# Half-length power tables, a last tile in two column halves, and the turning of six chunks of k moved from TensorE to the DMA queue

**Chip, cores, metric.** One core of one Trainium2 chip. The metric is device time of one execution in microseconds (us), given as the median of the runs of one kernel. Everything here is one core; over 1.5% above the fastest of the same kernel counts as slow. Runs of one batch ran on the same chip, beside runs of the kernel before.

## The reference, cut to what matters

```python
def _attn_ref(r, k, v, w, u):            # r, k, v: (4, 8, 768, 48) float32; w, u: (8, 48)
    for t in range(S):
        cur = einsum('bhd,bhe->bhde', u[None] * kt, vt)
        y[:, :, t] = einsum('bhd,bhde->bhe', rt, state + cur)
        state = w[None, :, :, None] * state + einsum('bhd,bhe->bhde', kt, vt)
# then, on x = y as (4, 768, 384):  x + relu(layernorm(x) * g @ w1) @ w2      (w1: 384 x 1536)
```

The recurrence is done in 24 chunks of 128 tokens. Within a chunk, r is scaled by rising powers of w and k by falling ones, so that one masked score product per chunk takes the place of the recurrence. For this the kernel makes tables of powers of w at its start. An MLP over each chunk ("tile") follows and gives TensorE most of its work.

## The kernel before: the parts that matter

The tables are made by scans (a running product), turned on TensorE, and copied to `Fr` (two tables for r) and `Fk` (for k):

```python
T = const.tile([P, CK, 2 * L], FP32, name="T")          # CK = 3, L = 128
T2 = const.tile([P, CK, L], FP32, name="T2")
ones = const.tile([P, L], FP32, name="ones")
w_r = const.tile([P, CK], FP32, name="w_r")
...
for kc in range(CK):
    powers(T[:, kc, L + 1 : 2 * L], w_c, kc)             # scan of 127
    nc.scalar.copy(out=T[:, kc, 0:L], in_=T[:, kc, L : 2 * L])
nc.vector.reciprocal(out=w_r[:], in_=w_c[:])
for kc in range(CK):
    powers(T2[:, kc], w_r, kc)                           # scan of 128
```

`const` is the first of several pools of tiles. The pools lie one behind the other on each partition, every tile rounded up to 32 bytes. The tiles that loads write come behind `const`:

```python
dst = (k_t if what == "k" else vf_t)[i] = ld.tile([P, H, D], FP32, name=what)
...
eng.dma_start(out=dst[:], in_=src[b, :, s0 : s0 + L, :].rearrange("h t d -> t h d"))   # 192-byte pieces
```

k is scaled, turned by four TensorE transposes, and copied out of PSUM; a routine that does the same by a DMA is there but not used (`KP = 24`). The order of all work is made at build time by a small list scheduler that gets a duration for each task; each engine then works in that fixed order. SyncE (SP) issues nearly all DMAs in its own fixed order: loads, stores, and the turns of the normalized tile `xn`.

```python
if i < KP:   # TK: 4 transposes on TensorE, then kT: a copy on ScalarE (or VectorE)
else:
    add(f"kT{i}", "SP", 1.25, lambda i=i: transpose_k_by_dma(i), [f"sck{i}"], ..., lands=3.0)
```

Of the kernel before, what the change touches and what calls it, by code (L numbers as in the profile page):

```python
# [9 lines left out]
FP32 = mybir.dt.float32  # L10
# [116 lines left out]
def kernel(  # L127
# [12 lines left out]
    nc = tc.nc  # L140
# [130 lines left out]
    T = const.tile([P, CK, 2 * L], FP32, name="T")  # L271
    T2 = const.tile([P, CK, L], FP32, name="T2")
    nc.vector.memset(T[:, :, L : L + 1], 1.0)
    ones = const.tile([P, L], FP32, name="ones")
    nc.vector.memset(ones[:], 1.0)
    w_r = const.tile([P, CK], FP32, name="w_r")

    def powers(out, base, kc):
        nc.vector.tensor_tensor_scan(
            out=out,  # L280
            data0=base[:, kc : kc + 1].to_broadcast([P, out.shape[1]]),
            data1=ones[:, : out.shape[1]],
            initial=1.0,
            op0=ALU.mult,
            op1=ALU.mult,
        )
# [5 lines left out]
    nc.vector.tensor_copy(out=w_c[:], in_=wps[:, :CK])  # L292
    for kc in range(CK):
        powers(T[:, kc, L + 1 : 2 * L], w_c, kc)
        nc.scalar.copy(out=T[:, kc, 0:L], in_=T[:, kc, L : 2 * L])
    nc.vector.reciprocal(out=w_r[:], in_=w_c[:])
    for kc in range(CK):
        powers(T2[:, kc], w_r, kc)
# [4 lines left out]
    LH = L // 2  # L303
    for j in range(3):
        fps = ps_h.tile([P, 512], FP32, name="hp") if j < 2 else ps.tile([P, 512], FP32, name="y")
        for kc in range(CK):
            src = T2[:, kc] if j == 2 else T[:, kc, j : 2 * L : 2]
            nc.tensor.transpose(out=fps[:, kc * P : (kc + 1) * P], in_=src, identity=ident_f[:])
        src = fps[:, :C].rearrange("p (h d) -> p h d", h=H)
        nc.scalar.copy(out=Fr[:, j] if j < 2 else Fk[:], in_=src)  # L310
# [89 lines left out]

    def evacuate_r(i, eng):
        e, c = divmod(i, 2)
        rT_t[i] = trp.tile([P, HP, P], BF16, name="rT", bufs=NRT)
        (eng.copy if eng is nc.scalar else eng.tensor_copy)(  # L404
            out=rT_t[i][:].rearrange("p q (t j) -> p q j t", j=2),
            in_=tp_t[e][:, :, c * LH : (c + 1) * LH].rearrange("p (j q) t -> p q j t", j=2),
        )
# [43 lines left out]
    def bonus_copy(i):  # L451
        cc_t[i] = sb2.tile([P, H], FP32, name="cc")
        nc.scalar.copy(out=cc_t[i][:], in_=s_t[i][:, C : C + H])  # L453
# [138 lines left out]
    KP = 24  # L592
# [19 lines left out]
    def ln_evacuate(i):  # L612
        g, j = tile_group[i]
        nc.scalar.copy(out=xT_t[g][:, :, j * P : (j + 1) * P], in_=tp_t[i][:, :CK, :])
# [62 lines left out]

    plan = Planner(
# [5 lines left out]
    add("scan", "DVE", 5.65, None, pri=99)  # L684
    add("Fr", "ACT", 5.9, None, pri=99)
    add("Fk", "ACT", 0.65, None, needs=["Fr"], pri=99)
# [36 lines left out]
    for i in range(NT):  # L723
# [8 lines left out]
        if not half:  # L732
            add(f"scrb{e}", "", 0.0, None, [], [("scr", e, 1)], pri=p0)
            for t in range(2):
                add(f"scr{e}{t}", "POOL", 1.1, lambda g, e=e, t=t: scale_r(e, t, g), [f"r{e}", "Fr", f"scrb{e}"], [],
                    [("r", e)], pri=p0, alt=[("DVE", 0.7)])
            add(f"TR{e}", "PE", 0.46, lambda e=e: transposes_r(e), [f"scr{e}0", f"scr{e}1"], [("tr", ("r", e), 2)],
# [7 lines left out]
        else:  # L745
            add(f"kT{i}", "SP", 1.25, lambda i=i: transpose_k_by_dma(i), [f"sck{i}"], [("kT", i, 2)], [("sck", i)], pri=80,
                load=0.67, lands=3.0)
# [11 lines left out]
        add(f"cp{i}", "ACT", 0.2, lambda i=i: bonus_copy(i), [f"cc{i}"], [("cc", i, 1)], [("s", i)], pri=p0 + 1)  # L759
# [32 lines left out]
        if i < LNP:  # L792
            add(f"ln{i}", "PE", 0.18, lambda i=i: ln_transposes(i), [f"xn{i}", f"xT{g}"], [("tr", ("l", i), 1)],
                [("xn", i)], pri=p0 + 2)
            add(f"lc{i}", "ACT", 0.5, lambda i=i: ln_evacuate(i), [f"ln{i}"], [], [("tr", ("l", i))], pri=p0 + 2)
        else:
            add(f"lc{i}", "SP", 1.2, lambda i=i: ln_by_dma(i), [f"xn{i}", f"xT{g}"], [], [("xn", i)], pri=90, load=0.5, lands=3.0)
        for m in range(NM):
# [55 lines left out]
```

## Time and profile before

| | before |
|---|---|
| median of 3 runs | 159.12 us (158.75 to 160.19) |
| span of the profiled run, granted clock | 155.6 us, 1.00 |
| TensorE busy from 7 to 91 us, while loads run | 80.0 of 84 us |
| TensorE busy from 91 to 124 us | 32.91 of 33 us |
| DMA share from 7 to 91 us / from 91 on | about 1.0 / 0.3 and less |

The page has two regimes. As long as loads run, the DMA engines are full and TensorE has holes, partly filled with dummy products (`keep_warm` in the code, 8.3 us of busy time between 7 and 33; what they do to the clock is not shown). Once the loads are done, TensorE is the bound and every microsecond of it counts. The lines for this are in the prediction.

### The profile page before, as it was taken

The page shows a single profiled execution, that of the slowest core. Times are in us where ns is not written, and L with a number is a line of the kernel's source. Part 1 is how long each engine was busy: PE and PEld are TensorE (multiplying, and loading weights), DVE is VectorE, ACT ScalarE, POOL GpSimd, SP SyncE. Part 2 cuts the span into 40 slices and gives each one's busy share as a digit, 9 for nine tenths or more (in the row PEclk, how much of TensorE's full clock was granted, in tenths as well). Part 3 has the DMA queues.
Part 4 walks back from the last instruction along what each step waited for, and adds up shares of the span by engine and source line. Part 5 has one row for each costly group of instructions (what it writes and reads, how often), then busy time and mean ns, then how long its engine had stood idle before and what let it go on. Part 6 is the DMA issues. An engine that isn't in the chain of part 4 may idle for free.

```text
span 155.6 us, 4634 instructions
## 1 busy us (share of the span) xinstructions
PE 146.1 (94%) x1851; PEld 114.7 (74%) x1851; DVE 116.7 (75%) x232; ACT 97.4 (63%) x217; POOL 86.1 (55%) x116
## 2 busy tenths in 40 slices
PE   5999999989999999989899969999999999999990
PEld 5789898858886787757668757787887777777650
DVE  5879999978898999888989779898989731101231
ACT  3577888967869576737977458676575554463100
POOL 7379697687829976795794849953542120000000
PEclk9999999999999999999999999999999999999999
DMA  4999999998999999999999969212121220111122
GB/s 101 239 235 326 355 183 274 377 242 188 250 218 244 218 215 184 233 219 185 196 220 191 208 112 228 78 30 76 44 62 51 80 71 5 51 55 51 51 101 101
DMA packets 75418, 25.46 MB, mean 164 GB/s; under 512 B 69632, under 2 KB 74246, under 8 KB 75398
## 3 DMA queue, kind: packets, MB, share of 16 engines
q1 hardware_dynamic: 72070, 23.21, 64.9%
q10 hardware_dynamic: 3232, 1.97, 4.1%
q8 instruction: 14, 0.23, 0.7%
q14 instruction: 6, 0.05, 0.1%
q0 software_dynamic: 96, 0.01, 0.1%
HBM read 18.88 MB, written 4.72 MB: 152 GB/s over the span
## 4 chain that ended last, share of the span: by engine, by line
PE 60%; DVE 12%; DMA 11%; issue 5%; POOL 5%; ACT 4%; SPq 1%; POOLq 0%; DVEq 0%; ACTq 0%
PE o L654 22%; PE hp L627 20%; DMA wst<-in_moe_w_ch_dram 6%; DMA v<-in_v_dram 5%; PE at L422 3%; PE o L268 3%; PE hp L654 3%; DVE A L432 2%; PE tr L399 2%; DVE x L538 2%; PE tr L384 2%; PE y L525 2%; POOL Vb L457 1%; POOL sc L369 1%; DVE w_sb L350 1%
## 5 line engine op out<-in xcount | busy, mean ns | idle before, releaser
L627 PE MATMUL hp<-xT,w_sb 128*128 128x256 bf16 (+1 forms) x540 | 57.6, 251 | 0.7 <-DMA xT<-xn 0.6
L654 PE MATMUL o<-w_sb,hT 128*128 128x384 bf16 x264 | 52.1, 326 | 0.0
L627 PEld LDWEIGHTS <-w_sb 128*128 128x128 bf16 x540 | 43.5, 98 | 8.2 <-DMA xT<-xn 0.8
L641 ACT ACTIVATE hT<-hp 128x512 bf16<-128x512 f32 x60 | 35.5, 598 | 18.0 <-PE hp L627 17.5
L654 PEld LDWEIGHTS <-hT 128*128 128x128 bf16 x288 | 26.2, 98 | 13.0
L664 DVE SCALAR_TENSOR_TENSOR ot<-o,rs,x 128x384 f32<-128x384 f32 x22 | 13.5, 612 | 22.2 <-PE o L654 22.2
L432 DVE TENSOR_TENSOR A<-at,mask 128x1024 bf16<-128x1024 f32 x24 | 29.2, 1215 | 0.5 <-PE at L422 0.5
L457 POOL TENSOR_TENSOR Vb<-v,cc 128x384 f32<-128x384 f32 x24 | 20.8, 867 | 8.3 <-ACT cc L453 8.3
L369 POOL TENSOR_TENSOR sc<-r,Fr 128x384 bf16<-128x384 f32 x18 | 20.1, 1125 | 7.1 <-ACT Fr L310 2.7
L366 POOL TENSOR_TENSOR sc<-k,Fk 128x384 bf16<-128x384 f32 x19 | 19.8, 1041 | 0.1
L388 ACT COPY kT<-tr 128x512 bf16<-128x512 bf16 x22 | 12.9, 586 | 4.7 <-PE tr L384 3.3
L565 ACT ACTIVATE sq<-x,sum 128x384 bf16<-128x384 f32 x24 | 14.6, 609 | 1.7 <-DVE x L538 1.6
L538 DVE SCALAR_TENSOR_TENSOR x<-y,Vb 128x384 f32<-128x384 f32 x24 | 13.2, 548 | 1.9 <-POOL Vb L457 1.6
L404 ACT COPY rT<-tr 128x512 bf16<-128x512 bf16 x17 | 11.8, 738 | 4.1 <-PE tr L399 2.5
L268 PE MATMUL o<-ident 128*128 128x128 bf16 x152 | 12.1, 233 | 1.6 <-DVE ident L243 1.6
L268 PEld LDWEIGHTS <-ident 128*128 128x128 bf16 x152 | 9.9, 104 | 1.9 <-DVE ident L243 1.6
L422 PE MATMUL at<-rT,kT 48*128 48x128 bf16 x192 | 9.5, 219 | 1.7 <-ACT kT L388 1.5
L643 DVE TENSOR_SCALAR hT<-hp 128x512 bf16<-128x512 f32 x12 | 8.2, 687 | 1.8 <-PE hp L627 1.7
L384 PE MATMUL tr<-ident,sc 128*128 128x128 bf16 x92 | 8.9, 219 | 0.5 <-DVE rT L404 0.5
L422 PEld LDWEIGHTS <-kT 48*128 48x128 bf16 x192 | 5.4, 94 | 5.4 <-ACT kT L388 3.2
L525 PE MATMUL y<-vv,A 128*128 128x48 bf16 x192 | 8.7, 183 | 0.4 <-DVE A L432 0.4
L556 ACT ACTIVATE xn<-x,sum 128x384 bf16<-128x384 f32 x13 | 8.0, 618 | 1.6 <-DVE x L538 1.4
(87 smaller groups left out, 193.3 us busy)
## 6 DMA issues: line engine op xcount, KB each, us to landing
r<-in_r_dram SPq DMA_DIRECT2D x12, 384.0 KB, 4.6
k<-in_k_dram SPq DMA_DIRECT2D x24, 192.0 KB, 4.4
wst<-in_moe_w_ch_dram SPq DMA_DIRECT2D x6, 768.0 KB, 7.2
v<-in_v_dram SPq DMA_DIRECT2D x22, 192.0 KB, 3.9
out_dram<-ot SPq DMA_DIRECT2D x16, 192.0 KB, 2.7
out_dram<-ot ACTq DMA_DIRECT2D x8, 192.0 KB, 1.9
v<-in_v_dram ACTq DMA_DIRECT2D x2, 192.0 KB, 3.7
xT<-xn SPq DMA_TRANSPOSE x16, 3.0
```

Of the source, the lines that this page charges most:

```text
L268: nc.tensor.matmul(out=warm[:, :P], lhsT=ident[:], rhs=ident[:], start=True, stop=True)
L366: eng.tensor_tensor(out=k_bufs[i % NSC][:, :, :D], in0=k_t[i][:], in1=Fk[:], op=ALU.mult)
L369: eng.tensor_tensor(out=r_bufs[e % NSR][:, j, :, :D], in0=r_t[e][:, :, j * D : (j + 1) * D], in1=Fr[:, j], op=ALU.mult)
L422: nc.tensor.matmul(out=at_t[i][:, par, p, :], lhsT=kT_t[i][p0 : p0 + D, p, :], rhs=rT_t[i][p0 : p0 + D, p, :], start=True, stop=True,)
L432: nc.vector.tensor_tensor(out=A_t[i][:].rearrange("p e q t -> p (e q) t"), in0=at_t[i][:].rearrange("p e q t -> p (e q) t"), in1=mask[:].u ...
L457: nc.gpsimd.tensor_tensor(out=Vb_t[i][:], in0=vf_t[i][:], in1=cc_t[i][:].unsqueeze(2).to_broadcast([P, H, D]), op=ALU.mult)
L538: nc.vector.scalar_tensor_tensor(out=x_t[i][:], in0=y_t[i][:, :C], scalar=1.0, in1=Vb_t[i][:].rearrange("p h d -> p (h d)"), op0=ALU.mult, ...
L565: nc.scalar.activation(out=sq[:], in_=x_t[i][:], func=ACT.Square, bias=sum_t[i][:], scale=-float(C), accum_out=sq_t[e][:, c : c + 1],)
L627: nc.tensor.matmul(out=hp[:, f * gw : (f + 1) * gw], lhsT=w1_sb[:, n, kc, fb * P : (fb + 1) * P], rhs=xT_t[g][:, kc, :gw], start=(kc == 0) ...
L641: nc.scalar.activation(out=out, in_=src, func=ACT.Relu)
L654: nc.tensor.matmul(out=o_t[i][:, :C], lhsT=hT_t[g][:, fk, j * P : (j + 1) * P], rhs=w2_sb[:, fk, :], start=(fk == 0), stop=(fk == FK - 1),)
L664: nc.vector.scalar_tensor_tensor(out=ot_t[i][:], in0=o_t[i][:, :C], scalar=rs_t[i // 2][:, i % 2 : i % 2 + 1], in1=x_t[i][:], op0=ALU.mult ...
```

## The change

The intent: shorter scans (63 or 64 elements on w squared, the other half of each table by one multiplication), a shorter last step (last tile in two halves of 192 columns), and 24 transposes fewer on TensorE (k of the last six chunks turned by DMA), planned with a DMA latency of 5.0 us rather than 3.0. Copies of bonus, turned tables and layer norm may now go to VectorE too. The core of the diff:

```diff
-    T = const.tile([P, CK, 2 * L], FP32, name="T")
-    T2 = const.tile([P, CK, L], FP32, name="T2")
+    LH = L // 2
+    T = [const.tile([P, CK, 2, LH], FP32, name=f"T{j}") for j in range(3)]
-    ones = const.tile([P, L], FP32, name="ones")
+    ones = const.tile([P, LH], FP32, name="ones")
-    w_r = const.tile([P, CK], FP32, name="w_r")
+    w_r = const.tile([P, 2, CK], FP32, name="w_r")
+    w_s = const.tile([P, CK], FP32, name="w_s")
...
+    nc.vector.tensor_tensor(out=w_s[:], in0=w_c[:], in1=w_c[:], op=ALU.mult)
     for kc in range(CK):
-        powers(T[:, kc, L + 1 : 2 * L], w_c, kc)
+        powers(T[0][:, kc, 0, 1:LH], w_s[:, kc : kc + 1])
+        nc.scalar.copy(out=T[0][:, kc, 1], in_=T[0][:, kc, 0])
+        nc.gpsimd.tensor_scalar(out=T[1][:, kc], in0=T[0][:, kc, 0:1]..., scalar1=w_c[:, kc : kc + 1], ...)
...
-    KP = 24
+    KP = 18
...
-                load=0.67, lands=3.0)
+                load=0.67, lands=5.0)
...
+        if i == NT - 1:
+            for h in range(2):
+                ... # dh: half products, oh: 128x192 add, sh: half store
```

More of the change, by code (lines that the diff above doesn't have):

```diff
@@ L268, in keep_warm, with powers @@
             nc.tensor.matmul(out=warm[:, :P], lhsT=ident[:], rhs=ident[:], start=True, stop=True)
-    T = const.tile([P, CK, 2 * L], FP32, name="T")
-    T2 = const.tile([P, CK, L], FP32, name="T2")
-    nc.vector.memset(T[:, :, L : L + 1], 1.0)
-    ones = const.tile([P, L], FP32, name="ones")
+    LH = L // 2
+    T = [const.tile([P, CK, 2, LH], FP32, name=f"T{j}") for j in range(3)]
+    nc.vector.memset(T[0][:, :, 0, 0:1], 1.0)
+    ones = const.tile([P, LH], FP32, name="ones")
     nc.vector.memset(ones[:], 1.0)
-    w_r = const.tile([P, CK], FP32, name="w_r")
-    def powers(out, base, kc):
+    w_r = const.tile([P, 2, CK], FP32, name="w_r")
+    w_s = const.tile([P, CK], FP32, name="w_s")
+    def powers(out, base):
+        n = out.shape[1]
         nc.vector.tensor_tensor_scan(
-            out=out,
-            data0=base[:, kc : kc + 1].to_broadcast([P, out.shape[1]]),
-            data1=ones[:, : out.shape[1]],
-            initial=1.0,
-            op0=ALU.mult,
-            op1=ALU.mult,
+            out=out, data0=base.to_broadcast([P, n]), data1=ones[:, :n], initial=1.0, op0=ALU.mult, op1=ALU.mult
         )
@@ L292 @@
     nc.vector.tensor_copy(out=w_c[:], in_=wps[:, :CK])
+    nc.vector.tensor_tensor(out=w_s[:], in0=w_c[:], in1=w_c[:], op=ALU.mult)
     for kc in range(CK):
-        powers(T[:, kc, L + 1 : 2 * L], w_c, kc)
-        nc.scalar.copy(out=T[:, kc, 0:L], in_=T[:, kc, L : 2 * L])
-    nc.vector.reciprocal(out=w_r[:], in_=w_c[:])
-    for kc in range(CK):
-        powers(T2[:, kc], w_r, kc)
+        powers(T[0][:, kc, 0, 1:LH], w_s[:, kc : kc + 1])
+        nc.scalar.copy(out=T[0][:, kc, 1], in_=T[0][:, kc, 0])
+        nc.gpsimd.tensor_scalar(
+            out=T[1][:, kc],
+            in0=T[0][:, kc, 0:1].to_broadcast([P, 2, LH]),
+            scalar1=w_c[:, kc : kc + 1],
+            scalar2=None,
+            op0=ALU.mult,
+        )
+    nc.vector.reciprocal(out=w_r[:, 0], in_=w_c[:])
+    nc.vector.tensor_tensor(out=w_r[:, 1], in0=w_r[:, 0], in1=w_r[:, 0], op=ALU.mult)
+    for kc in range(CK):
+        t2 = T[2][:, kc].rearrange("p e t -> p (e t)")
+        powers(t2[:, 1:L:2], w_r[:, 1, kc : kc + 1])
+        nc.vector.tensor_scalar(
+            out=t2[:, 0:L:2], in0=t2[:, 1:L:2], scalar1=w_c[:, kc : kc + 1], scalar2=None, op0=ALU.mult
+        )
     keep_warm(10)
@@ L302, with copy_table @@
     Fk = const.tile([P, H, D], FP32, name="Fk")
-    LH = L // 2
+    tab = []
     for j in range(3):
-        fps = ps_h.tile([P, 512], FP32, name="hp") if j < 2 else ps.tile([P, 512], FP32, name="y")
+        tab.append(ps_h.tile([P, 512], FP32, name="hp") if j < 2 else ps.tile([P, 512], FP32, name="y"))
         for kc in range(CK):
-            src = T2[:, kc] if j == 2 else T[:, kc, j : 2 * L : 2]
-            nc.tensor.transpose(out=fps[:, kc * P : (kc + 1) * P], in_=src, identity=ident_f[:])
-        src = fps[:, :C].rearrange("p (h d) -> p h d", h=H)
-        nc.scalar.copy(out=Fr[:, j] if j < 2 else Fk[:], in_=src)
+            src = T[j][:, kc].rearrange("p e t -> p (e t)")
+            nc.tensor.transpose(out=tab[j][:, kc * P : (kc + 1) * P], in_=src, identity=ident_f[:])
+    def copy_table(j, eng):
+        src = tab[j][:, :C].rearrange("p (h d) -> p h d", h=H)
+        (eng.copy if eng is nc.scalar else eng.tensor_copy)(out=Fr[:, j] if j < 2 else Fk[:], in_=src)
     vec = const.tile([P, NR], FP32, name="vec")
@@ L449, in bonus, with bonus_copy @@
             )
-    def bonus_copy(i):
+    def bonus_copy(i, eng):
         cc_t[i] = sb2.tile([P, H], FP32, name="cc")
-        nc.scalar.copy(out=cc_t[i][:], in_=s_t[i][:, C : C + H])
+        (eng.copy if eng is nc.scalar else eng.tensor_copy)(out=cc_t[i][:], in_=s_t[i][:, C : C + H])
     def bonus_value(i):
@@ L610, in ln_by_dma, with ln_evacuate @@
         nc.sync.dma_start_transpose(out=xT_t[g][:, :, j * P : (j + 1) * P], in_=xn_t[i][:])
-    def ln_evacuate(i):
+    def ln_evacuate(i, eng):
         g, j = tile_group[i]
-        nc.scalar.copy(out=xT_t[g][:, :, j * P : (j + 1) * P], in_=tp_t[i][:, :CK, :])
+        (eng.copy if eng is nc.scalar else eng.tensor_copy)(out=xT_t[g][:, :, j * P : (j + 1) * P], in_=tp_t[i][:, :CK, :])
     hp_t = {}
@@ L675, in store, with down_half, finish_half, store_half @@
         eng.dma_start(out=out[b, c * L : (c + 1) * L, :], in_=ot_t[i][:])
+    CH = C // 2
+    oh_t, oth_t = {}, {}
+    def down_half(h, m):
+        g, j = tile_group[NT - 1]
+        if m == 0:
+            oh_t[h] = ps_h.tile([P, 512], FP32, name="hp")
+        for fk in range(m * PM, (m + 1) * PM):
+            nc.tensor.matmul(
+                out=oh_t[h][:, :CH],
+                lhsT=hT_t[g][:, fk, j * P : (j + 1) * P],
+                rhs=w2_sb[:, fk, h * CH : (h + 1) * CH],
+                start=(fk == 0),
+                stop=(fk == FK - 1),
+            )
+    def finish_half(h):
+        i = NT - 1
+        oth_t[h] = sb2.tile([P, CH], FP32, name="oth")
+        nc.vector.scalar_tensor_tensor(
+            out=oth_t[h][:],
+            in0=oh_t[h][:, :CH],
+            scalar=rs_t[i // 2][:, i % 2 : i % 2 + 1],
+            in1=x_t[i][:, h * CH : (h + 1) * CH],
+            op0=ALU.mult,
+            op1=ALU.add,
+        )
+    def store_half(h, eng):
+        b, c = divmod(NT - 1, NCH)
+        eng.dma_start(out=out[b, c * L : (c + 1) * L, h * CH : (h + 1) * CH], in_=oth_t[h][:])
     plan = Planner(
@@ L683 @@
     NU = {g: FK * n * P // 512 for g, n in enumerate(group_len)}
-    add("scan", "DVE", 5.65, None, pri=99)
-    add("Fr", "ACT", 5.9, None, pri=99)
-    add("Fk", "ACT", 0.65, None, needs=["Fr"], pri=99)
+    add("scan", "DVE", 5.3, None, pri=99)
+    add("first", "ACT", 4.7, None, pri=99)
+    add("rows0", "POOL", 4.9, None, pri=99)
+    for j, (name, done, bank_) in enumerate((("Fr0", 5.0, "hp"), ("Fr1", 5.5, "hp"), ("Fk", 6.0, "y"))):
+        add(f"t{name}", "", done, None, pri=99, takes=[(bank_, ("t", j), 1)])
+        add(name, "ACT", 0.5, lambda e, j=j: copy_table(j, e), [f"t{name}"], gives=[(bank_, ("t", j))], pri=99 - j, alt=[("DVE", 0.48)])
     for name, lands in (("r0", 5.4), ("k0", 6.4), ("v0", 7.5), ("rows", 5.5)):
@@ L734 @@
             for t in range(2):
-                add(f"scr{e}{t}", "POOL", 1.1, lambda g, e=e, t=t: scale_r(e, t, g), [f"r{e}", "Fr", f"scrb{e}"], [],
+                add(f"scr{e}{t}", "POOL", 1.1, lambda g, e=e, t=t: scale_r(e, t, g), [f"r{e}", f"Fr{t}", f"scrb{e}"], [],
                     [("r", e)], pri=p0, alt=[("DVE", 0.7)])
-            add(f"TR{e}", "PE", 0.46, lambda e=e: transposes_r(e), [f"scr{e}0", f"scr{e}1"], [("tr", ("r", e), 2)],
+            add(f"TR{e}", "PE", 0.46, lambda e=e: transposes_r(e), [f"scr{e}0", f"scr{e}1"] + ([f"TK{i - 1}"] if QP < i < KP else []), [("tr", ("r", e), 2)],
                 [("scr", e)], pri=p0)
@@ L758 @@
             [("q", i)], pri=p0 + 1)
-        add(f"cp{i}", "ACT", 0.2, lambda i=i: bonus_copy(i), [f"cc{i}"], [("cc", i, 1)], [("s", i)], pri=p0 + 1)
+        add(f"cp{i}", "ACT", 0.2, lambda e, i=i: bonus_copy(i, e), [f"cc{i}"], [("cc", i, 1)], [("s", i)], pri=p0 + 1, alt=[("DVE", 0.15)])
         add(f"Vb{i}", "POOL", 0.85, lambda i=i: bonus_value(i), [f"cp{i}", f"v{i}"], [("Vb", i, 1)],
@@ L794 @@
                 [("xn", i)], pri=p0 + 2)
-            add(f"lc{i}", "ACT", 0.5, lambda i=i: ln_evacuate(i), [f"ln{i}"], [], [("tr", ("l", i))], pri=p0 + 2)
+            add(f"lc{i}", "ACT", 0.5, lambda e, i=i: ln_evacuate(i, e), [f"ln{i}"], [], [("tr", ("l", i))], pri=p0 + 2, alt=[("DVE", 0.36)])
         else:
             add(f"lc{i}", "SP", 1.2, lambda i=i: ln_by_dma(i), [f"xn{i}", f"xT{g}"], [], [("xn", i)], pri=90, load=0.5, lands=3.0)
+        if i == NT - 1:
+            for h in range(2):
+                for m in range(NM):
+                    add(f"dh{h}{m}", "PE", 0.34, lambda h=h, m=m: down_half(h, m),
+                        [f"re{g}_{u}" for u in range(NU[g])] + ([f"dh{h}{m - 1}"] if m else [f"dh0{NM - 1}"] if h else []),
+                        [("hp", ("oh", h), 1)] if m == 0 else [], [("hT", g)] if m == NM - 1 and h else [], pri=-40, kind="d")
+                add(f"oh{h}", "DVE", 0.38, lambda h=h: finish_half(h), [f"dh{h}{NM - 1}", f"rs{i // 2}"], [],
+                    [("hp", ("oh", h))] + ([("x", i)] if h else []), pri=99)
+                add(f"sh{h}", "SP", 0.55, lambda e, h=h: store_half(h, e), [f"oh{h}"], pri=99, load=0.3, lands=1.8,
+                    alt=[("ACT", 0.5)])
+            continue
         for m in range(NM):
```

## The prediction

> **What bounds the kernel now.** I read the page first, then busy time in five stretches, then the timeline of TensorE at its stalls and at the end, and last the timeline around the one stall over 1 us.
>
> The first fence is busy time by engine in five stretches (columns: start:end, length, PE, PEld, DVE, ACT and POOL busy with instruction counts, granted clock, DMA share, GB/s).
>
> ```profile
> 7.00:33.00 26.00, 25.38 (x451) 22.10 (x448) 23.86 (x46) 20.20 (x46) 20.82 (x27) 1.00 1.09 288
> 33.00:60.00 27.00, 26.24 (x368) 20.70 (x368) 25.20 (x48) 20.68 (x47) 19.65 (x25) 1.00 1.06 223
> 60.00:91.00 31.00, 28.39 (x376) 21.69 (x370) 26.00 (x48) 21.25 (x53) 23.92 (x31) 1.00 0.97 198
> 91.00:124.00 33.00, 32.91 (x412) 25.77 (x413) 30.30 (x59) 21.36 (x48) 17.14 (x23) 1.00 0.32 82
> 124.00:152.00 28.00, 27.81 (x204) 19.71 (x202) 6.20 (x11) 10.26 (x18) 0.89 (x2) 1.00 0.16 56
> ```
>
> Up to 91 us the DMA engines are full (share about 1) and TensorE has holes: 2.6 us idle between 60 and 91, and between 7 and 33 part of its busy time is the dummy matmuls[...]. From 91 us the loads are nearly over and TensorE is 99.6% busy. So there are two regimes: a loading part, where what TensorE loses is time waiting for data in a fixed instruction order, and a part of 61 us where each TensorE microsecond removed is a microsecond of the result. Three groups of the page price what the change touches:
>
> ```profile
> L388 ACT COPY kT<-tr 128x512 bf16<-128x512 bf16 x22 | 12.9, 586 | 4.7 <-PE tr L384 3.3
> L268 PE MATMUL o<-ident 128*128 128x128 bf16 x152 | 12.1, 233 | 1.6 <-DVE ident L243 1.6
> ...
> L384 PE MATMUL tr<-ident,sc 128*128 128x128 bf16 x92 | 8.9, 219 | 0.5 <-DVE rT L404 0.5
> ```
>
> The mean of a pipelined matmul (219 ns) is not its price; spacing is. The timeline gives it: four k transposes start at 57.84 and the next group starts at 58.07.
>
> ```profile
> 57.84 0.39 PE L384 MATMUL tr<-ident,sc 128*128 128x128 bf16 x4
> 58.07 0.81 PE L654 MATMUL o<-w_sb,hT 128*128 128x384 bf16 x4
> ```
>
> That is 0.23 us for a chunk. By the same reading an up group takes 0.66, a third of a down product 0.65, an r pair 0.44. Last, the one long stall and the end of the program:
>
> ```profile
> 86.40 0.59 ACT L388 COPY kT<-tr 128x512 bf16<-128x512 bf16 x1
> ...
> 89.93 0.51 ACT L375 CAST vv<-v 128x384 bf16<-128x384 f32 x1 [2.34 <-DMA v<-in_v_dram]
> 90.35 0.16 ACT L453 COPY cc<-s 128x8 f32<-128x8 f32 x1
> 90.40 0.59 ACT L388 COPY kT<-tr 128x512 bf16<-128x512 bf16 x1
> ```
> ```profile
> 91.05 0.40 PE L422 MATMUL at<-rT,kT 48*128 48x128 bf16 x8 [1.33 <-ACT kT L388]
> ```
> ```profile
> 148.40 2.11 PE L654 MATMUL o<-w_sb,hT 128*128 128x384 bf16 x12
> 150.35 1.46 PE L654 MATMUL hp<-w_sb,hT 128*128 128x384 bf16 x8
> 150.60 0.62 DVE L664 SCALAR_TENSOR_TENSOR ot<-o,rs,x 128x384 f32<-128x384 f32 x1 [2.04 <-PE o L654]
> 151.85 0.62 DVE L664 SCALAR_TENSOR_TENSOR ot<-hp,rs,x 128x384 f32<-128x384 f32 x1 [0.63 <-PE hp L654]
> ```
>
> ScalarE sat 2.34 us behind a v load, the copy of kT stood behind it in ScalarE's order, and TensorE lost 1.33 us. The end is one full tile's residual add (0.62), then 155.6 - 152.47 = 3.1 us for the store and the closing.
>
> [...]three scans of 127 elements take 1.05 us, 0.35 each[...]. [...]scaling k on VectorE takes 0.55 us alone and 1.08 at 6.74 us, when GpSimd scales r. [...]a DMA can turn 2-byte data[...]; the 16 of this kernel, all from SP, land after 3.0 us in the median. [...]this trace has 0.23 / 4 = 57 ns, and I use that.
>
> **The change, part by part.**
>
> Tables at the start. Before: six scans, 1.05 + 1.06, and a 0.15 reciprocal, VectorE from 3.50 to 5.71. After: a product of w with itself and of its reciprocal (about 0.15 each, like the reciprocal), six scans of 63 or 64[...], one reciprocal 0.15, three multiplications of 64 that replace half the inverse table[...]. Sum 2.15 against 2.21: nearly nothing[...]. The odd table is now made by three GpSimd multiplications, alongside. The copies split: Fr0 and Fk on ScalarE, Fr1 on VectorE after its tables (about 5.6 to 6.1), so scaling r, second half, can begin on GpSimd at 6.1 where it began at 6.41; the first r scaling on VectorE stays near 6.0 to 6.1. Gain 0.2 us (0 to 0.4).
>
> Dummy matmuls and early balance. Built, the program has 140 instead of 152 dummies; those after the first r transposes go from 112 to 98. At 56 ns that is 0.8 us less filler, but a dummy fills a wait that the plan foresees, so it is a gain only where data is there. VectorE is 23.9 of 26 us busy between 7 and 33. By the order, up to the fifth chunk it loses eight casts and scalings of weights and gets copies and centring in their place, a net relief of about 3 us by the durations of the rows (w_sb 0.4 to 0.8, hT 0.68, against cc 0.17, xn 0.41, xT 0.4). In particular no w2 cast stands on it any more, which had held it 1.03 us at 32.48. But weights and v still land when the full DMA queues bring them. I count 0.7 us of gain for both.
>
> k by DMA for chunks 18 to 23. All of it lies after 91 us. TensorE: 6 x 0.23 = 1.35 us off, a full gain. ScalarE (5) and VectorE (1) lose the kT copies, 6 x 0.59 = 3.5 us. Products q of these chunks now read kT in SBUF: two on VectorE (0.52 rather than 0.41), four on GpSimd (1.15 each), which has 17 of 33 us busy. Added are six DMA transposes, one third larger than the others: about 4 us to land, planned with 5.0. The share of DMA is 0.1 to 0.2 after 100 us, so only the first one or two meet loads. In the order, the score product of chunk 18 stands after several down and up groups and r is turned early for both last pairs, so I count no stall.
>
> Last tile in two halves. Residual add and store of the last tile would be shortened if it came last. The order says that it does not: after the 24 half products (192 columns), TensorE does the whole product of tile 22 (12 x 384 columns), and the last VectorE instruction before the end is a 128x384 add. So the end stays one full add and one full store: 0.62 + 3.1, as now. The half products cost 24 x 0.08 = 1.95 us, the same columns as 12 x 0.163. Gain 0.0 (between -0.2 and 0.1).
>
> The stalls between 60 and 91. The v cast that held ScalarE in front of kT of chunk 17 is now on GpSimd; another v cast, of chunk 20, stands in front of it instead, whose load is issued about 5 us earlier. I give 0.6 of the 1.33 us back as gain, less 0.4 for new waits of the same kind elsewhere.
>
> Sum: 0.2 + 0.7 + 1.35 + 0.0 + 0.2 = 2.45 us. 159.12 - 2.45 = 156.7.
>
> **The rivals.** First, the loads are the bound until 91 us, so all that is won earlier is given back as waiting. For it: a share near 1 from 7 to 91, and waits on v loads of 12.1 us over its casts. Against: TensorE has a stock of MLP products in the loading part (down products of tile 9 stand beside the attention of chunk 17), so its holes come from the fixed order and not from lack of work. It would leave only the 1.35: 157.8. Second, the new latency replaces the old work: SP issues in order, a DMA turn of k behind a turn of xn or a store that is not ready waits with it, and scores stall. For it: SP waited up to 5.6 us with a turn of xn for room. Against: by the order each such wait is for something planned well before. At 0.5 us for three chunks it eats the gain: 158.2. Third, the early relief of VectorE carries fully and the 91 us stall goes: 0.2 + 2 + 1.35 + 1.2 = 4.75, so 154.4.
>
> **Range and chances.** The certain part is 1.35. The reshuffled order in the loading part has a spread of about 1.3 us, since the idle time of TensorE there is several us and any of it may move. That gives 155.0 to 158.4 for 8 in 10. Faster by over 2% means below 155.94, a gain of 3.2: 0.30. Slower by over 2% needs above 162.3: 0.02. The rest, 0.68, is within 2%.
>
> **What would show it.** Right: TensorE over 99% busy from the score product of chunk 18 on, kT turns landing in 3 to 5 us with no wait on them; k transposes on TensorE 24 x 4 down to 18 x 4; the last VectorE instruction a 128x384 add, and some 3.1 us from its end to the end of the span; [...]first r transposes at most 0.4 earlier. Wrong: holes of over 0.5 us before score products of the last six chunks; a tail shorter by 0.3 or more; TensorE idle plus filler up to 91 us changed by more than 2 us either way, which would be the most likely cause of a miss.

## More of the kernel before

One more view is needed as a base for later, the transfers between 3 and 33 us (q1 is the queue of SP; columns: packets, MB, time of the packets as a share of 16 engines; the second line is the loads of k, with the median from issue to landing in us):

```profile
q1 hardware_dynamic: 18059, 8.33, 108.7%
...
k<-in_k_dram SPq DMA_DIRECT2D x6, 192.0 KB, 4.8
```

From the first line one gets the mean time of a packet: 30 us x 16 engines x 1.087 / 18059 = 28.9 ns, over packets of all sizes on this queue.

## The result, and the profile after

| | before | after |
|---|---|---|
| median | 159.28 us (4 runs) | 164.62 us (4 runs, 164.16 to 164.91) |
| ratio, 95% interval | 1 | 1.0326 [1.0271, 1.0381] |
| span of the profiled run | 155.6 us | 163.1 us |

The change made the kernel slower by 3.3%; the prediction said 1.5% faster. Ratios here and below are the mean time of one kernel's fast runs over that of the other's of the same rounds, so they are not quite the ratio of the medians.

Busy time in the same five stretches as in the prediction, kernel after (columns: stretch, length, PE, PEld, DVE, ACT, POOL busy, granted clock, DMA share, GB/s):

```profile
7.00:33.00 26.00, 24.76 (x420) 22.32 (x419) 23.15 (x45) 17.93 (x40) 21.91 (x27) 1.00 1.08 279
33.00:60.00 27.00, 26.17 (x379) 20.65 (x378) 24.35 (x49) 19.49 (x44) 21.74 (x28) 1.00 1.01 214
60.00:91.00 31.00, 27.05 (x346) 20.61 (x345) 27.03 (x52) 20.86 (x49) 21.93 (x26) 1.00 0.97 188
91.00:124.00 33.00, 30.54 (x357) 22.91 (x355) 25.93 (x49) 18.37 (x42) 17.79 (x22) 0.95 0.58 117
124.00:152.00 28.00, 28.00 (x248) 20.94 (x247) 10.62 (x19) 12.73 (x27) 4.83 (x7) 1.00 0.17 54
```

Read the last column first: 279, 214 and 188 GB/s where the kernel before had 288, 223 and 198, at nearly the same DMA share (1.08, 1.01 and 0.97 against 1.09, 1.06 and 0.97). TensorE lost 1.3 us more between 60 and 91, and 2.4 us more between 91 and 124, where the prediction counted no stall at all; there the granted clock is 0.95. The transfers between 3 and 33 us, kernel after:

```profile
q1 hardware_dynamic: 17091, 8.01, 108.6%
...
k<-in_k_dram SPq DMA_DIRECT2D x6, 192.0 KB, 5.3
```

That is 30 x 16 x 1.086 / 17091 = 30.5 ns a packet, against 28.9.

The stall after 91 us shows in the timeline (start, duration, engine, line, operation; in brackets the idle time before it and what ended it):

```profile
96.81 2.46 SPq L405 DMA_TRANSPOSE kT<-sc  x1
99.36 0.54 SPq L195 DMA_DIRECT2D v<-in_v_dram  x1
...
102.69 0.36 DVE L388 CAST vv<-v 128x384 bf16<-128x384 f32 x1 [3.78 <-DMA v<-in_v_dram]
...
104.04 0.42 DVE L429 TENSOR_TENSOR q<-rT,kT 128x512 bf16<-128x512 bf16 x1
...
104.51 0.25 PE L456 MATMUL s<-uwI,q 128*128 128x2 bf16 x4 [2.31 <-DVE q L429]
```

The last load of v (chunk 23) stands on SP behind the first DMA turn of k, and is issued at 99.36; in the kernel before ScalarE had issued it at 91.4. The cast of that v is on VectorE ahead of the product q of chunk 18. VectorE sat 3.78 us for a v that is needed five chunks later, and TensorE 2.31 us for q. After the hole the granted clock fell to 0.5 for 3.4 us:

```profile
105.00:110.00 5.00, 5.00 (x41) 3.81 (x38) 3.20 (x8) 2.69 (x6) 1.79 (x2) 0.66 0.44 103
```

The start did not get earlier either. The first score products, kernel before and then kernel after, with the three GpSimd multiplications of the new tables:

```profile
9.08 0.40 PE L422 MATMUL at<-rT,kT 48*128 48x128 bf16 x8
```
```profile
4.10 1.84 POOL L294 TENSOR_SCALAR T<-T,w_c 128x128 f32<-128x128 f32 x3 [0.36 <-DVE T L281]
...
11.05 0.40 PE L436 MATMUL at<-rT,kT 48*128 48x128 bf16 x8
```

They are 1.97 us late. Part of this is chance: in this run the clock was granted in full only from 9.8 us on (20 dummy products from 6.91 us took 2.34 us, where 18 from 5.93 us took 1.17 in the kernel before). In runs of the same start with the clock granted in full earlier (18 dummy products in 1.17 us in b_new_tables) they come at 9.92 to 9.94, 0.84 to 0.86 late. The second r table waits for GpSimd until 5.94. Its copy stands on VectorE behind the new multiplications (done at 6.25) and starts at 6.51, and the first scaling of r behind it starts at 6.99, where it started at 5.97.

The end is as predicted, one full 128x384 add, then 163.1 - 159.93 = 3.2 us:

```profile
159.31 0.62 DVE L678 SCALAR_TENSOR_TENSOR ot<-o,rs,x 128x384 f32<-128x384 f32 x1 [1.53 <-PE o L668]
```

Further waits of TensorE, before and then after, without one of 1.6 us at the very start that both have (waited for: total us, times, longest):

```profile
PE at L422 <- ACT kT L388: 1.5, 2, 1.3
PE hp L627 <- DMA xT<-xn: 0.6, 1, 0.6
```
```profile
PE y L539 <- DVE A L446: 2.8, 5, 1.2
PE s L456 <- DVE q L429: 2.5, 2, 2.3
...
PE at L436 <- ACT kT L401: 1.3, 1, 1.3
```

### The profile page after: what moved, and what is told of

It is laid out like the page before. It is cut to its first block, busy times and chain, and to the rows that moved or that the text cites. A ratio compares the mean times of both kernels' runs of the same rounds, so it can differ in the third digit from the quotient of the medians.

```text
span 163.1 us, 4594 instructions
## 1 busy us (share of the span) xinstructions
PE 149.1 (91%) x1827; PEld 116.6 (71%) x1827; DVE 118.9 (73%) x243; ACT 92.0 (56%) x203; POOL 93.1 (57%) x122
## 4 chain that ended last, share of the span: by engine, by line
PE 40%; DVE 18%; DMA 16%; POOL 15%; issue 6%; ACT 1%; SPq 1%; POOLq 0%; DVEq 0%
PE hp L641 14%; PE o L668 13%; DMA v<-in_v_dram 12%; DVE A L446 5%; POOL Vb L471 4%; POOL sc L382 3%; PE o L268 3%; DMA r<-in_r_dram 3%; POOL sc L379 2%; DVE x L552 2%; DVE ot L678 2%; POOL vv L388 1%; DVE rT L418 1%; DMA xT<-xn 1%; DVE Z L511 1%
## 5 line engine op out<-in xcount | busy, mean ns | idle before, releaser
L641 PE MATMUL hp<-xT,w_sb 128*128 128x256 bf16 (+1 forms) x540 | 58.6, 253 | 0.3 <-DVE hT L657 0.2
L668 PE MATMUL o<-w_sb,hT 128*128 128x384 bf16 x264 | 53.0, 328 | 0.2 <-DVE ot L678 0.2
L655 ACT ACTIVATE hT<-hp 128x512 bf16<-128x512 f32 x62 | 36.7, 596 | 24.0 <-PE hp L641 23.7
L382 POOL TENSOR_TENSOR sc<-r,Fr 128x384 bf16<-128x384 f32 x17 | 18.8, 1113 | 4.0 <-DMA r<-in_r_dram 1.8
L379 POOL TENSOR_TENSOR sc<-k,Fk 128x384 bf16<-128x384 f32 x16 | 17.4, 1086 | 0.0
L418 ACT COPY rT<-tr 128x512 bf16<-128x512 bf16 x18 | 12.5, 735 | 5.8 <-PE tr L412 3.7
L388 POOL CAST vv<-v 128x384 bf16<-128x384 f32 x11 | 6.4, 584 | 6.2 <-DMA v<-in_v_dram 6.2
L511 DVE TENSOR_TENSOR Z<-S,WLZ 128x384 bf16<-128x384 f32 x11 | 9.9, 897 | 0.0
L539 PEld LDWEIGHTS <-A 128*128 128x128 bf16 x192 | 7.0, 97 | 4.0 <-DVE A L446 3.7
L657 DVE TENSOR_SCALAR hT<-hp 128x512 bf16<-128x512 f32 x10 | 6.8, 684 | 4.0 <-PE hp L641 3.9
```

Source lines behind the costliest of these rows:

```text
L379: eng.tensor_tensor(out=k_bufs[i % NSC][:, :, :D], in0=k_t[i][:], in1=Fk[:], op=ALU.mult)
L382: eng.tensor_tensor(out=r_bufs[e % NSR][:, j, :, :D], in0=r_t[e][:, :, j * D : (j + 1) * D], in1=Fr[:, j], op=ALU.mult)
L539: nc.tensor.matmul(out=y[:, h * D : (h + 1) * D], lhsT=A_t[i][:, par, p, :], rhs=v_t[i][:, h, :], start=first, stop=True, skip_group_check ...
L641: nc.tensor.matmul(out=hp[:, f * gw : (f + 1) * gw], lhsT=w1_sb[:, n, kc, fb * P : (fb + 1) * P], rhs=xT_t[g][:, kc, :gw], start=(kc == 0) ...
L655: nc.scalar.activation(out=out, in_=src, func=ACT.Relu)
L668: nc.tensor.matmul(out=o_t[i][:, :C], lhsT=hT_t[g][:, fk, j * P : (j + 1) * P], rhs=w2_sb[:, fk, :], start=(fk == 0), stop=(fk == FK - 1),)
```

## The experiments

There were 18 runs, in five batches. In all of them the order of the remaining work was frozen: the plan of the kernel in question was taken as it is and only the named task moved, so that the scheduler could not reshuffle the rest. In the short diffs, `put(x, y)` takes task x out of this fixed order and puts it right behind task y.

### First batch: undo one part, or do one part alone

**a_old_tables**: the changed kernel with the table code of the kernel before.

> The changed kernel with the tables of the kernel before put back, and the planned order of every other instruction kept as the changed kernel has it. In the traces the first r transposes start at 9.04 us after the change and at 6.93 before. Theory 1 (the new start costs its 2.0 us to the end): the first transposes at about 7.0, the score product of chunk 5 near 32 instead of 34.2, and 162.6 us in all (164.6 - 2.0). Rival (the full DMA queues are the bound until 95 us and hide the start): chunk 18 at the same 101 us, and 164.4 or more.

160.12 us, ratio 1.0107 [1.0028, 1.0186] (three fast runs, one slow). Two thirds of the loss goes away, more than the 2.0 us of the theory.

**a_cast_later**: the changed kernel with one task moved.

```diff
+    put("vc23", "A20")     # the cast of v of chunk 23 behind the masked product of chunk 20
```

> The changed kernel with one instruction moved in VectorE's order: the cast of the last v chunk stands behind the masking of chunk 20 instead of in front of the product q of chunk 18. Theory 2 (this cast, waiting for a load that lands at 102.7 us, holds q of chunk 18, empties TensorE for 2.3 us, and the pause costs 3.4 us at half clock, 1.7 more): no hole before the bonus product of chunk 18, no record of half clock between 100 and 110 us, 160.6 to 161.5 us. Rival (the lateness is of the loads, another instruction then waits as long): a hole of 2 us moves to another place and the time stays above 163.8.

161.69 us, 1.0213 [1.0142, 1.0284], so the cast was worth 1.1 points; the time is just above the expected range, and far below the 163.8 of the rival. Where the hole had been, the profile of this run has the bonus product standing right behind its work, and the clock stays at 1.00 between 105 and 110:

```profile
101.81 0.24 PE L456 MATMUL s<-uwI,q 128*128 128x2 bf16 x4
...
105.00:110.00 5.00, 5.00 (x67) 3.75 (x65) 3.85 (x9) 2.33 (x7) 2.15 (x3) 1.00 0.64 102
```

**b_new_tables**: the kernel before with the new tables and nothing else.

> The kernel before with the new tables alone, its planned order kept. Theory 1: first r transposes near 9 us, 161.2 us (159.3 + 2.0). Rival (hidden behind loads): 159.0 to 159.8. My own prediction said 159.1, 0.2 less.

162.18 us, 1.0223 [1.0166, 1.0281]. The tables alone cost 3.5 us, though they delay the first scores by 0.84 us only.

**b_k_dma**: the kernel before with k of chunks 18 to 23 turned by DMA right behind the scaling.

```diff
+    for i in range(18, NT):
+        seq.remove(by[f"TK{i}"])
+        by[f"kT{i}"].update(fn=lambda i=i: transpose_k_by_dma(i), alt=None)
+        put(f"kT{i}", f"sck{i}")
```

> The kernel before with k of the last six chunks turned by DMA alone, each DMA right behind the scaling of its k, everything else in its planned order. Prediction's term: 6 x 0.23 = 1.35 us less on TensorE, 157.9 us. Rival (the DMA turns wait in SP's order behind turns of xn and come late, so the scores wait): holes of TensorE before the score products of chunks 18 to 23 and 159.3 or more.

157.13 us, 0.9919 [0.9867, 0.9971]: about 1.3 us (0.5 to 2.1 by the interval), in line with the 1.35 of the prediction. The view of the tile kT shows the six turns and their landing (ns to issue; us to landing, min/median/max):

```profile
L392 SPq DMA_TRANSPOSE kT<-sc x6: 1190/1212/1796, 94.3 to 110.1; - x6
...
DMA to landing us min/median/max: 2.4/3.0/3.4
```

My theory after this batch was that the late start grows on its way: the score products of b_new_tables were 0.84 us late for chunk 0, 1.8 for chunk 8, 3.9 for chunk 10 and 4.4 for chunk 17, and SP's loads, which stand behind stores and turns, were late too (k of chunk 10 was issued 2.4 us late, k of chunk 17 3.5).

### Second batch: both repairs, the two small parts, and a pure delay

**a_both**: old tables and the moved cast.

> The changed kernel with both repairs: the old power tables and the cast of v of chunk 23 moved behind the masked product of chunk 20 on VectorE. Theory: the two losses have separate causes (a late start that grows through the loading part; a cast in front of q of chunk 18) and add up: 1.0326 less 2.2 points less 1.1 points, so a ratio of 0.999 to before, between 0.994 and 1.003, and no wait of TensorE over 1 us after 95 us. Rival: they overlap, because without the late start the load of v of chunk 23 would be issued earlier and its cast would not wait; then both together give no more than the old tables alone: 1.009 to 1.011.

158.82 us, 0.9952 [0.9876, 1.0027]. At this placement of the tiles the two losses add up, within the noise; what is left is a gain of half a per cent that is not told apart from nothing (three fast runs of six). The profiled run is slow, so no times are read from its trace.

**b_delay**: the kernel before with two more scans ahead of the tables, and no new instruction elsewhere.

```diff
+    for kc in range(2):
+        powers(T2[:, kc, 1:], w_c, kc)
     for kc in range(CK):
         powers(T[:, kc, L + 1 : 2 * L], w_c, kc)
```

> The kernel before with nothing changed but two scans of 127 ahead of the tables on VectorE, into the inverse table that is overwritten later: the start is some 0.7 us late, with no new GpSimd work[...]. Theory: a late start is not absorbed and not only passed on, but grows on its way through the loading part (stores and turns in SP's order hold back later loads), so the scores of chunk 0 are 0.6 to 0.8 late, those of chunk 10 and on 2 to 4, and the time grows by 2 to 3.3 us, ratio 1.013 to 1.021. First rival: it is passed on as it is, plus 0.7 us, 1.0045. Second rival: it is absorbed by the full DMA queues, ratio below 1.002, and what the new tables cost is from the GpSimd multiplications and their order.

158.99 us, 1.0020 [0.9975, 1.0065]. The theory fell. In the profiled run the delay came out larger than meant: the first scaling of r is 0.62 us late, and the rest goes with the clock, which was granted in full only from 9.4 us on in this run. The larger part of the delay was gone at the end. The score products of chunk 0 and chunk 23 in this run:

```profile
10.85 0.40 PE L424 MATMUL at<-rT,kT 48*128 48x128 bf16 x8
...
120.18 0.40 PE L424 MATMUL at<-rT,kT 48*128 48x128 bf16 x8
```

and chunk 23 in the kernel before:

```profile
119.54 0.40 PE L422 MATMUL at<-rT,kT 48*128 48x128 bf16 x8
```

1.77 us late at the start, 0.64 at the end. What is left is about what the edit put in, so the trace rather shows a delay passed on; the first rival's 1.0045 lies inside the interval, and so do values below 1.002 as the second expected; the two are not told apart. The theory that a late start grows to 1.013 or more is out. So the new tables did something else that is worse than being late.

**b_halves** and **b_k_dma_halves**: the last tile in two halves, now really last, without and with the DMA turns.

```diff
+    seq.append(last_tile)      # half products, half add, half store, twice, behind all other work
```

> The kernel before with only the last tile in two column halves, and these really at the end of the program, behind the whole product of tile 22. Theory: the last add shrinks from 0.62 to 0.41 us and the last store is half as large, so 0.2 to 0.4 us earlier, ratio 0.9975 to 0.9985 and about 2.9 to 3.1 us from the end of the last add to the end of the span. Rival: the end is fixed cost alone and the narrower products cost what the add saves: no difference, ratio 0.9995 to 1.001.

158.42 us, 0.9977 [0.9930, 1.0025], as expected in size but not told apart from nothing. The two last adds of this run:

```profile
152.46 0.42 DVE L697 SCALAR_TENSOR_TENSOR oth<-hp,rs,x 128x192 f32<-128x192 f32 x1 [0.32 <-PE hp L686]
153.45 0.42 DVE L697 SCALAR_TENSOR_TENSOR oth<-hp,rs,x 128x192 f32<-128x192 f32 x1 [0.57 <-PE hp L686]
```

The add is 0.2 us shorter than the full one, and the span ends 156.7 - 153.87 = 2.8 us after it, where it was 3.1.

> The kernel before with k of chunks 18 to 23 turned by DMA right behind the scaling, and the two halves of the last tile at the end. Theory: the gains add: 0.992 (k by DMA, measured alone) times 0.998 (halves, estimated), a ratio of 0.990, between 0.986 and 0.993, about 156.8 us; it would beat both kernels. Rival: halves give nothing: 0.992 as before.

156.79 us, 0.9905 [0.9847, 0.9963].

### Third batch: which piece of the new tables?

Three theories: G, the GpSimd multiplications; A, the placement of the buffers behind the tables; C, the order of the copies.

**b_tables_dve** (multiplications on VectorE) and **b_pool_mults** (old tables, the same three multiplications by GpSimd into a spare tile):

```diff
-        nc.gpsimd.tensor_scalar(out=T[1][:, kc], ...
+        nc.vector.tensor_scalar(out=T[1][:, kc], ...
```

> The kernel before with the new tables, as measured at 1.0223, but the three multiplications that make the odd table on VectorE instead of GpSimd. A late start of 1.77 us alone cost nothing measurable (1.002), so something else in the new tables must cost 3.5 us. Theory G: the GpSimd multiplications, which run from 4.1 to 5.9 us while the first loads are issued, are the cause: a ratio of 1.000 to 1.007, and the loads of k, v and weights are issued up to 10 us as in the kernel before (at most 0.3 us later, against 0.64 with GpSimd). Theory A: it is the new tiles' sizes, which move every later buffer by 232 bytes: ratio 1.018 to 1.026 as before. Theory C: it is the order of the copies at the start (odd table by VectorE): 1.018 to 1.026 too.

163.36 us, 1.0249 [1.0146, 1.0351].

> The kernel before with its old tables, and three multiplications of 128x128 by GpSimd at the same time into a spare tile that nobody reads. Theory G (GpSimd's work at the start is the cause[...]): ratio 1.012 to 1.025, early loads 0.5 us or more later by 10 us. Theories A and C: 0.999 to 1.004.

158.10 us, 0.9962 [0.9868, 1.0056]. Theory G fell by both.

**b_tables_fr_act**: the new tables with all copies on ScalarE.

> The kernel before with the new tables, all three copies of the turned tables on ScalarE as in the kernel before. Theory C (order of the copies): ratio 0.999 to 1.008. Theories G and A: 1.018 to 1.026.

161.14 us, 1.0159 [1.0086, 1.0231]. The interval overlaps that of the new tables as they are, and most of the loss stays; theory C fell as the main cause.

**b_tables_pad**: the new tables with one tile made longer, to put the later buffers back.

```diff
-    ones = const.tile([P, LH], FP32, name="ones")
+    ones = const.tile([P, LH + 58], FP32, name="ones")
```

> The kernel before with the new tables, and one tile made 232 bytes longer, so that every later buffer lies where it lay in the kernel before. Theory A (placement): ratio 0.999 to 1.006. Theories G and C: 1.018 to 1.026, as measured for the new tables without it.

162.22 us, 1.0230 [1.0156, 1.0303]. It looked as if theory A had fallen too, and nothing was left. But the control was wrong: I had added up the tiles by their sizes, and they are rounded up to 32 bytes. In the built program this kernel's k tile starts 32 bytes higher than in the kernel before, not at the same place.

What put me on it was the speed of the loads. Between 3 and 10 us the DMA moved 229 or 230 GB/s in all six traces with new tables, and 246 or 247 in all eight with old ones, whatever else the kernel did. Since pieces, queue and issue order are the same, I looked up in the built programs where the tiles start (the traces hold no addresses):

| kernel | first k tile at byte | past a multiple of 64 | past a multiple of 256 |
|---|---|---|---|
| before, and the seven other kernels with old tables | 56768 (58304 in b_pool_mults) | 0 | 192 |
| after, a_cast_later, b_new_tables, b_tables_dve, b_tables_fr_act | 56544 | 32 | 224 |
| b_tables_pad | 56800 | 32 | 224 |

The new tables are 224 bytes smaller: 256 less for the shorter `ones`, 32 more for `w_s`. The tiles of k, v, r, the weights and the stores all move by these 224 bytes.

### Fourth batch: 32 bytes

**b_misaligned**: the kernel before with one tile 32 bytes longer and no instruction changed.

```diff
-    ones = const.tile([P, L], FP32, name="ones")
+    ones = const.tile([P, L + 8], FP32, name="ones")
```

> The kernel before with one edit and no instruction changed: the table of ones is 32 bytes longer, so that the tiles that loads write start 32 bytes past a multiple of 64. Theory P: packets of the loads take 22 to 23 ns between 3 and 20 us, the second megabyte lands at 11.1 to 11.3 us instead of 10.4, and the time grows as with the new tables: ratio 1.012 to 1.025. Rival T: 0.998 to 1.003 and packets of 20 ns.

162.97 us, 1.0260 [1.0201, 1.0319]. This is the cause, by itself. The transfers of this run between 3 and 33 us:

```profile
q1 hardware_dynamic: 17499, 8.13, 109.5%
...
k<-in_k_dram SPq DMA_DIRECT2D x6, 192.0 KB, 5.9
```

30.0 ns a packet, and 5.9 us for a load of k where it took 4.8. As expected, the second megabyte had landed at 11.16 us instead of 10.39 (from the packet records of the traces). The score product of chunk 0 is on time (9.06 us), that of chunk 10 is 2.4 us late and that of chunk 23 3.8. The compute instructions did not change: the up product is 251 ns (mean of its two shapes), the masked product 1216 against 1215, relu 598, as before. What grew are waits of TensorE for what comes from loads, k at 2.7 us in all against 1.5, and weights at 1.5, a wait that the kernel before does not have:

```profile
PE at L422 <- ACT kT L388: 2.7, 2, 2.0
...
PE hp L627 <- POOL w_sb L350: 1.5, 1, 1.5
```

A part of the 2.6% goes with the clock. Four of the six runs had a granted clock of 0.987 to 0.989 and took 162.8 to 163.3 us. The other two, with 0.998 and 1.000, took 161.22 and 161.47, about 1.7% above the mean of 158.7 of the kernel before's fast runs, none of which had a low clock. The kept trace is one of these two; it has a hole of 1.96 us before the score product of chunk 17 and no fall of the clock. In b_tables_dve, whose clock was 0.986, a hole of 2.54 us at the same place is followed by 3.41 us at half clock. That the low-clock runs here lost time in the same way is likely, but their traces were not kept.

**a_aligned**: the changed kernel with `ones` 32 bytes longer (k tile at 56576, a multiple of 64 and of 256).

> The changed kernel with one edit: a table of ones is 32 bytes longer, so every later buffer starts 32 bytes higher, and the tiles that loads write (r, k, v, weights) start at a multiple of 64 bytes again, as in the kernel before; in all six runs with the new tables they started at 32 more than one, also in the run that was meant to restore the placement. Theory P (placement modulo 64 bytes slows the loads): the time of a packet of the loads between 3 and 20 us falls from 22 to 23 ns to 19 to 21, the second megabyte has landed by 10.6 us instead of 11.2, and the ratio to before falls from 1.0326 to 1.005 to 1.015, as with the old tables. Rival T (something in the tables' instructions themselves): packets stay at 22 to 23 ns and the ratio at 1.028 to 1.036.

158.92 us, 0.9991 [0.9930, 1.0052]. 32 bytes in one table take away the whole loss of 3.3%, more than expected, which fits that the new place is better than that of the kernel before too (fifth batch). The trace still has the hole before the bonus product of chunk 18, now of 1.51 us, and no fall of the clock after it.

**b_tables_aligned**: the kernel before with the new tables and the 32 bytes.

> The kernel before with the new tables and the table of ones 32 bytes longer, so that loads write to multiples of 64 bytes. Theory P: the late start by 0.84 us stays and is absorbed as a delay of 1.77 us was, so ratio 0.998 to 1.006 against 1.0223 without the edit. Rival T: 1.018 to 1.026.

157.36 us, 0.9910 [0.9858, 0.9963], better than expected. The profiled run is slow, so no times are read from its trace.

**a_aligned_cast**: the changed kernel with the 32 bytes and the moved cast.

> The changed kernel with the 32 bytes, and with the cast of v of chunk 23 moved behind the masked product of chunk 20. Theory: both losses are repaired, and what the change was meant to give is left: ratio 0.990 to 1.000, about as the run with old tables and the moved cast (0.9952). Rival: the new tables still cost what they cost at the start (0.84 us), ratio 1.002 to 1.008.

158.22 us, 0.9949 [0.9893, 1.0005]. At this placement moving the cast gains 0.4 points, which is not told apart from nothing.

### Fifth batch: finer placement, and the parts put together

**b_align512**: the kernel before with `ones` 64 bytes longer, so that the first k tile starts at 56832, a multiple of 512, and all load tiles at a multiple of 256. Again no instruction changes.

```diff
-    ones = const.tile([P, L], FP32, name="ones")
+    ones = const.tile([P, L + 16], FP32, name="ones")
```

> The kernel before with one edit and no instruction changed: the table of ones 64 bytes longer. The loads' tiles, which start 192 bytes past a multiple of 256 in the kernel before, then start at a multiple of 256. Theory L[...]: packets of the loads of r at 384 bytes and of weights shorter by a tenth or more, those of k and v at 192 bytes unchanged, and the ratio 0.988 to 0.998. Rival M (only the multiple of 64 counts): packets as in the kernel before, ratio 0.998 to 1.002; what the new tables gained at 0.991 would then be the tables' own.

156.75 us, 0.9889 [0.9815, 0.9962]. It beats both kernels without an instruction touched. The transfers between 3 and 33 us:

```profile
q1 hardware_dynamic: 18465, 8.46, 100.8%
...
k<-in_k_dram SPq DMA_DIRECT2D x6, 192.0 KB, 4.6
```

26.2 ns a packet. So three placements give three speeds: 30.0 ns (32 past a multiple of 64), 28.9 (0 past 64, 192 past 256), 26.2 (0 past 256). The other traces fall in with them: 30.3 to 30.8 ns in the six with new tables of the first three batches, 28.1 to 29.3 in the eight placed as before, 26.2 to 26.5 in the five at a multiple of 256. This fits b_tables_aligned: its 0.991 is about the placement's gain, and nothing is left that these runs could put down to the new tables themselves.

The gain is shown for the order of the kernel before. In the changed order the same step bought 1.2 points with the cast in place (a_aligned, with new tables, against a_old_tables) and nothing with the cast moved (0.9949 in a_aligned_cast, 0.9952 in a_both). Why is open.

By size of the pieces (means over the first 60 us, worked out from the records of the traces): 192-byte pieces of k and v took 17.5, 16.3 and 15.5 ns in these three, the 384-byte pieces of r 27.8, 26.0 and 23.6. Over all twenty traces the three groups do not overlap: 17.1 to 17.9, 16.1 to 16.3 and 15.5 to 15.6 for k and v, 26.9 to 28.7, 25.2 to 26.0 and 22.9 to 23.6 for r. The 2048-byte pieces of w1 show no such order, 90 to 96 ns everywhere. The r pieces differ between the two worse placements too (27.8 against 26.0), and k pieces between the two better ones (16.3 against 15.5). So theory L, which expected a tenth less for r and the weights and no change for k and v, holds for r at best. The effect is shown; what causes it is not.

**b_all**: new tables with the 32 bytes, k by DMA, halves last.

> The parts that paid, put together on the kernel before: new tables with the 32 bytes (0.991 alone), k of chunks 18 to 23 by DMA right behind the scaling (0.992 alone) and the last tile's halves at the very end (0.998 alone). If they add up: 0.981, between 0.977 and 0.986, about 155.8 us, faster than both kernels. Rival: the gain of the placement lies in the loading part and ends in a wait of the later part, as it did in the profile of the run with the tables alone (chunk 18's scores 1.9 us late), so only 0.985 to 0.991.

157.14 us, 0.9904 [0.9840, 0.9969]. The parts do not add up: 0.981 was expected and lies outside. In its trace a packet takes 26.2 ns, as in b_align512, but the scores of chunk 10 are 2.45 us later than in the kernel before (0.77 in b_align512), and TensorE waits 2.0 us in two score products for a kT copy on ScalarE (1.1 us there). The rival had said 0.985 to 0.991, with a wait in the later part. That a fixed order tuned for slower loads does not use faster ones at every point would fit; it was not tried, and stays open.

## Why the prediction was wrong, by its own steps

**The step that failed** is the one under "Tables at the start", with the sentence "Sum 2.15 against 2.21: nearly nothing". It priced the tables by their instructions alone, and the 2.15 was the estimate: no trace had shown how long the shorter scans and the multiplications take. Even these were mis-sized: the three multiplications took 0.26 to 0.30 us each, the last three scans, of 64 elements, 285 ns in the mean where those of 128 had taken 408, so VectorE needed 2.75 us (3.50 to 6.25) where it had needed 2.21. But this cost nothing that the times could show: new tables at a good placement give 0.991, and the placement alone 0.989. What did cost is that the tables also lie in front of a long row of tiles, and that by becoming 224 bytes shorter they moved every load tile off a multiple of 64 bytes. The sum has no term for that, and neither has a rival: all of them take the speed of the loads as given. Its size is 2.6% by itself (b_misaligned; 1.7% in its two full-clock runs), about 4 us where the whole predicted gain was 2.45. The prediction even named the place, "a loading part, where what TensorE loses is time waiting for data", and built nothing on it.

**Gain 0.2 at the start** had the wrong sign: the first scores were 0.84 us later, because the second r table comes from GpSimd at 5.94 us and its copy stands behind VectorE's longer work. It cost little: a delay at this place, 0.62 us by the edit and 1.77 in the profiled run, gave 1.002, and at most 1.0065 by its interval.

**"I count no stall"** for the last six chunks was the second failure: TensorE stood for 2.31 us in front of chunk 18. It was worth 1.1 points at the placement of the changed kernel (a_cast_later), 1.6 at that of the kernel before (a_both against a_old_tables) and 0.4 at the best one (a_aligned_cast against a_aligned), each with an uncertainty of more than half a point. The order was read for where the DMA turns stand, not for what they push back: the last v load behind them on SP, and its cast ahead of q on VectorE. The second rival had the mechanism, "SP issues in order, a DMA turn of k behind a turn of xn or a store that is not ready waits with it", but looked at the turn as the victim; the victim was a load behind the turn.

**k by DMA, 1.35 us** (6 x 0.23 is 1.38): right in size. Alone it gave about 1.3 us, and the turns landed in 3.0 us in the median where about 4 was expected.

**Last tile in halves, 0.0**: right. The last add is a full one, 0.62 us, and some 3.2 us follow. Where the halves really are last the tail is 0.5 us shorter, a gain that the times could not tell from zero.

**Dummies and early balance, 0.7, and stalls between 60 and 91, 0.2**: not shown. With the losses repaired the changed kernel is at 0.995 on either way (a_both, a_aligned_cast), where k by DMA alone gives 0.992; these runs cannot tell the two apart, so no gain or loss of the re-planned order is shown.

**The first rival**, the loads are the bound until 91 us, was nearer than the main line. It drew the conclusion that gains are lost there, and not the other one, that whatever changes the loads' speed moves the result.

The account of the 3.26 points, then: old tables take away 2.2 (placement as before), moving the cast 1.6 on top of it, and half a per cent of gain is left, within the noise.

## What to carry to other kernels

When a change alters the size of any tile, compare where the DMA tiles start in the two builds before pricing instructions: here 32 bytes of one small table were worth 2.6%, and starting load tiles at a multiple of 256 gave the kernel before 1.1% for no work. Where loads are the bound, put the mean time of a packet (share x engines x window / packets) into the table of what you look at. And when a control says that a cause is out, check that the control did what it was meant to do: the padded kernel that cleared the placement had moved the tiles to another bad place.

## What the runs show of the hardware

- **Speed by start address of a DMA's SBUF side.** Over all packets of the loading queue between 3 and 33 us: 30.0 ns a packet at 32 past a multiple of 64 (b_misaligned), 28.9 at a multiple of 64 that is 192 past a multiple of 256 (before), 26.2 at a multiple of 256 (b_align512); 1.026, 1 and 0.989 of the time of the kernel. Pieces of 192 and 384 bytes show it (17.5, 16.3 and 15.5 ns; 27.8, 26.0 and 23.6), pieces of 2048 do not (90 to 96 ns everywhere).
- **Clock after a hole.** Holes of TensorE of 1.72, 2.31 and 2.54 us in three runs (2.31 in the kernel after, 2.54 in b_tables_dve) were each followed by 3.41 us at half clock, and holes of 1.9 to 2.1 us in four others (1.96 in b_misaligned, 1.9 in b_new_tables) were not: in these seven the length alone does not decide.
- **Latency of a DMA transpose.** A 128x512 bf16 turn from SBUF to SBUF landed after 2.4 to 3.4 us, median 3.0, in b_k_dma, and after up to 6.1 us, median 3.3, in b_all.
